# Two layers of linear attention and MLP on one core: program order from loops replaced by order from a table

## The chip, the cores and the metric

The kernel runs on 1 core of one Trainium2 chip. The metric is the device time of one execution in microseconds (us), as the median of several runs. Times inside an execution come from one execution that the hardware profiler recorded. The engines are named as the profile names them: PE (TensorE, its matmuls) and PEld (its weight loads), DVE (VectorE), ACT (ScalarE), POOL (GpSimd), SP (SyncE, which here issues DMAs). Every engine works off its own instructions in the order of the program, and waits for the others where it needs their data or their buffers.

## The reference, cut to what matters

Two layers follow each other. Each is an attention part and an MLP part, with S = 2048 rows, D = 448 columns, 16 heads of 28 and F = 1792 hidden columns, all in f32.

```python
def attention(x, wqkv, wo):                # x: 2048 x 448
    q, k, v = heads(x @ wqkv)              # 16 heads of 28
    phi = lambda t: where(t > 0, t + 1, exp(t)) + 1e-6
    pq, pk = phi(q), phi(k)
    kv = einsum("bhsd,bhse->bhde", pk, v)  # one 28 x 28 matrix a head
    z = einsum("bhsd->bhd", pk)
    num = einsum("bhqd,bhde->bhqe", pq, kv)
    den = einsum("bhqd,bhd->bhq", pq, z)[..., None] + 1e-6
    return merge(num / den) @ wo

def mlp(x, w1, b1, w2, b2):
    return gelu(x @ w1 + b1) @ w2 + b2

for layer in range(2):
    x = x + attention(layernorm(x), wqkv, wo)
    x = x + mlp(layernorm(x), w1, b1, w2, b2)
```

## The kernel before, in words

**Precision.** PE multiplies float32r operands. To keep f32 precision every operand is split into a high part (a rounded copy, on ACT: xh, kh, qh, yh, gh) and a low part (the difference, on DVE or POOL: xl, kl, ql, yl, gl), and each product is three matmuls: high by high, high by low, low by high. So every step of PE has a chain of a copy and a subtraction ahead of it.

**Tiles.** Rows are worked on in 16 tiles of 128. The first stage of a layer does for each tile t: statistics of the layer norm on DVE (`ln_stats`, L188 to L192), their inverse root on POOL (L194), the normalization on DVE (L367), and the transposition of the tile. The first 6 tiles of layer 0 are transposed on PE (`transpose_x`, L239: T0 to T5; the last 64 columns come doubled from a "tail" copy on ACT, L371); the others go through 32 x 32 transposes on DVE, a store of two tiles to DRAM as a square (`store_sq`, sq_a) and four DMAs that read it back spread out (`spread`, sp). The transposed tile is split (XH, XL). Then PE makes the key projection K(t) (`proj`, L290 to L294, 11 matmuls of 448 columns, into one of two banks "m") and the query projection Q(t) (the same lines, banks "h"). phi is relu and exp on ACT and a combination on DVE (L300 to L303). Queries are stored to DRAM (pq_d). Keys are split (kh L419, kl L420) and added up for z (za, L424). G(t) (`stage_g`, L446 to L450, 11 matmuls) adds x^T k of the tile to four banks "acc"; from the sum G the matrices kv are made later, so the values v are never formed row by row.

**Order of the first stage.** A string of tokens per tile sets the order (STEP, and STEP_0 for tile 0): `STEP = "a qp K T X s n G kp tu kh bg Q sp"`, with G one tile late, so that on PE it reads K(t), T(t+1), G(t-1), Q(t). In layer 0 this begins K0 T1 Q0 K1 T2 G0 Q1. Beside it the weights of the MLP are loaded and split in 30 background pieces (`bg_pieces`, 24 of them in this stage of layer 0, with their low halves on POOL).

**Crossing to the MLP.** When G is complete, the string ORDER sets one sequence: the last Q and G(15), z, the copies of G (gt, L558 and L560), kv (`trans_kv`), its masking, the product with wo (m), its split (Mh, Ml), and for the four tiles of block 0 the division by the denominator, the transposition (tq), the product with M (o), the residual, the layer norm and its transposition. The queries 10 to 15 (Q) are spread between these as filling for PE: Q10 stands ahead of the last G, the others behind it.

**MLP.** Four tiles make a block of 512 rows; there are four blocks of 14 steps. Step i of a block is f(i) (`mlp1`: 11 matmuls of 512 columns, L716 to L720, then gelu on ACT L722, the copy gh L725 and the subtraction gl L726) and y(i) (`mlp2`: 12 matmuls of 448 columns, L734 to L736). The loop emits f(i+1) ahead of y(i), from f(0). At the start of block 0 `trans_chunks` copies M by 14 small DMAs on SP into the place of the query weights (the step called mc in the changed kernel). The strings PLAN_0, PLAN_1 and PLAN put the attention of the next block behind these steps, among them one product oc (11 matmuls, L668 to L671) for each tile. In the last block of layer 0, the weights and the first tiles of layer 1 are prepared (steps 2 to 12).

**Buffers.** Every kind of tile has a ring of buffers (9 for x, 5 halves "S" for squares and loads, 3 for "e", 2 for most others), and the banks of PSUM are 4 "acc", 2 "h" and 2 "m"; who waits for a buffer follows from the order of the program.

Of the kernel before, what the change touches and what calls it, by code (L numbers as in the profile page):

```python
# [12 lines left out]
OP = mybir.AluOpType  # L13

# [8 lines left out]
def linear_attn_mlp_kernel(  # L23
# [19 lines left out]
    NB = NT // 4  # L43
# [11 lines left out]

    def dram(shape, dt, name):
        return tc.dram_tile(shape, dt, name=name)

# [3 lines left out]
    def bank(tag, bufs, name):  # L62
        return psum.tile([128, 512], F32, name=name, tag=tag, bufs=bufs)

    NH = 9

    def t448(tag, bufs, name, dt=F32):
        bufs = NH if tag == "H" else bufs
        return work.tile([128, D], dt, name=name, tag=tag, bufs=bufs)

    def t512(tag, bufs, name, dt=F32):
        return work.tile([128, 512], dt, name=name, tag=tag, bufs=bufs)

    def f(ap):
        return ap.bitcast(F32)


    xt = {}

    def load_x(l, t):  # L80
        xt[l, t] = t448("H", 8, f"x{l}_{t}")
        sp.dma_start(xt[l, t], x_d[l][t * 128:(t + 1) * 128, :])

    load_x(0, 0)

    wkq = {}

    def stage_piece(src, c, eng, s):

        if c < 3:  # L90
            eng.dma_start(s, src[c * 128:(c + 1) * 128, :])
        else:
            eng.dma_start(s[0:64], src[TL:D, :])
            eng.dma_start(s[64:128], src[TL:D, :])
        return s

    def load_kq(name, col):
        src = wqkv[:, col:col + D]
        st = [work.tile([128, 1024], F32, name="stg", tag="S", bufs=5) for h in range(2)]
        return [stage_piece(src, c, (sp, act)[c % 2], st[c // 2][:, c % 2 * 512:c % 2 * 512 + D]) for c in range(4)]  # L100

    def stage_square(src):

        st = []
        for h in range(2):
            s = work.tile([128, 1024], F32, name="stg", tag="S", bufs=5)[:, :2 * D]
            s = s.rearrange("p (c n) -> p c n", c=2)
            if h == 0:
                sp.dma_start(s, src[:256, :].rearrange("(c p) n -> p c n", p=128))
            else:  # L110
                sp.dma_start(s[:, 0], src[256:TL, :])
                sp.dma_start(s[:64, 1], src[TL:, :])
                sp.dma_start(s[64:, 1], src[TL:, :])
            st += [s[:, 0], s[:, 1]]
        return st

    def piece(name, i):
        return t448(f"{'W' if name == 'k' else 'V'}{i}", 1, f"w{name}{i}", F32R)

    def split_hi(name, c, st):  # L120

        if c < 3:
            wkq[name, c] = piece(name, c), piece(name, 3 + c)
            act.copy(wkq[name, c][0], st[c])
        else:
            wkq[name, 3] = piece(name, 6)
            tmps[name] = t512("e", 3, "sx", F32R)[:, :D]
            act.copy(tmps[name][64:128], st[3][64:128])
            act.copy(wkq[name, 3][0:64], st[3][0:64])

    tmps = {}

    def split_lo(name, c, st):

        eng = pool if c == 1 else dve
        if c < 3:
            hi, lo = wkq[name, c]
            eng.tensor_tensor(lo, st[c], f(hi), op=OP.subtract)
        else:
            eng.tensor_tensor(wkq[name, 3][64:128], st[3][64:128], f(tmps.pop(name)[64:128]), op=OP.subtract)  # L140

    def split_piece(name, c, st):
        split_hi(name, c, st)
        split_lo(name, c, st)

    def split_kq(name, st):
        for c in range(4):
            split_piece(name, c, st)

    st_k = load_kq("k", D)  # L150
    load_x(0, 1)
    st_q = load_kq("q", 0)
    load_x(0, 2)


    ident = consts.tile([128, 128], F32, name="ident")
    make_identity(nc, ident)
    warm = bank("m", 2, "warm")
    for i in range(20):
        pe.transpose(warm[:, :128], ident, ident)  # L160
    mhalf = consts.tile([128, 1], F32, name="mhalf")
    pool.memset(mhalf, -0.5)
    tiny = consts.tile([128, 1], F32, name="tiny")
# [20 lines left out]


    def ln_stats(xs):
        st = work.tile([128, 6], F32, name="bst", tag="bst", bufs=2)
        dve.bn_stats(st, xs)  # L188
        mv = work.tile([128, 2], F32, name="bmv", tag="bmv", bufs=2)
        dve.bn_aggr(mv, st)  # L190
        ve = work.tile([128, 1], F32, name="bve", tag="bve", bufs=2)
        dve.tensor_scalar(ve, mv[:, 1:2], 1e-5, None, op0=OP.add)  # L192
        rs = work.tile([128, 1], F32, name="brs", tag="brs", bufs=2)
        pool.tensor_tensor(rs, ve, mhalf, op=OP.pow)  # L194
        return xs, mv, rs

    def ln_norm(stats, name, twice=True):

        xs, mv, rs = stats
        xn = t512("xn", 2, name)  # L200
        dve.tensor_scalar(xn[:, :D], xs, mv[:, 0:1], rs, op0=OP.subtract, op1=OP.mult)  # L201
        if twice:
            dve.tensor_scalar(xn[:, D:], xs[:, TL:], mv[:, 0:1], rs, op0=OP.subtract, op1=OP.mult)
        return xn

    class Block:
        def __init__(self):
            self.hi = work.tile([128, 2048], F32R, name="XH", tag="XH", bufs=2)  # L210
            self.lo = work.tile([128, 2048], F32R, name="XL", tag="XL", bufs=2)

        def pieces(self, t):

            s = slice(t * 512, (t + 1) * 512)
            return self.hi[:, s], self.lo[:, s]

        def moving(self, x, c):

            return x.rearrange("p (t c n) -> p t c n", t=4, c=4)[:, :, c]  # L220

        def still(self, x, t, c):

            return x[:, (t * 4 + c) * 128:(t * 4 + c + 1) * 128]

    blocks = {}

    def block(key):
        if key not in blocks:
            blocks[key] = Block()  # L230
        return blocks[key]

    tps = {}

    def transpose_x(xn, key, j, tail=None, tag="m"):
        block(key)
        tp = tps[key, j] = bank(tag, 2, "tp")
        for c in range(4):
            pe.transpose(tp[:, c * 128:(c + 1) * 128],  # L239
                         tail if tail is not None and c == 3 else xn[:, c * 128:(c + 1) * 128], ident)  # L240

    def split_x(key, j):
        tp = tps.pop((key, j))
        hi, lo = blocks[key].pieces(j)
        act.copy(hi, tp)
        dve.tensor_sub(lo, tp, f(hi))

    squares, stored, spreads = {}, {}, {}

    def half(name):
        return work.tile([128, 1024], F32, name=name, tag="S", bufs=5)

    def turn(x, key, t):
        x = x[:, :D]
        if (key, t // 2) not in squares:
            squares[key, t // 2] = half("sq")  # L260
        sq = squares[key, t // 2].rearrange("p (m c u n) -> p c m u n", m=4, c=4, n=32)[:, :, :, t % 2]
# [4 lines left out]
    def store_sq(key, h):  # L266
        d = stored[key, h] = dram([128, 1024], F32, f"sq_{'_'.join(map(str, key))}_{h}")
        sp.dma_start(d, squares.pop((key, h)))

    def spread(key, h):  # L270
        r = spreads[key, h] = half("sp")
        d = stored.pop((key, h)).rearrange("(i r) (m f) -> m r i f", i=4, m=4)
# [3 lines left out]
    def split_t(key, t, hi, lo):  # L276

        x = spreads[key, t // 2].rearrange("p (i c u n) -> p u c i n", i=4, c=4, n=32)[:, t % 2]
        h = hi.rearrange("p (c i n) -> p c i n", c=4, n=32)
        act.copy(h, x)  # L280
        dve.tensor_sub(lo.rearrange("p (c i n) -> p c i n", c=4, n=32), x, f(h))  # L281


    def proj(name, key, j):
        ps = bank("m" if name == "k" else "h", 2, "ps" + name)
        o = ps[:, :D]
        b = blocks[key]
        for c in range(3):
            hi, lo = wkq[name, c]
            pe.matmul(o, b.still(b.hi, j, c), hi, start=(c == 0), stop=False)  # L290
            pe.matmul(o, b.still(b.hi, j, c), lo, start=False, stop=False)  # L291
            pe.matmul(o, b.still(b.lo, j, c), hi, start=False, stop=False)  # L292
        pe.matmul(o, b.still(b.hi, j, 3), wkq[name, 3], start=False, stop=False)
        pe.matmul(o, b.still(b.lo, j, 3), wkq[name, 3], start=False, stop=True)  # L294
        return o

    def phi(o, name, into=None):

        e = t512("e", 3, name)[:, :D]
# [151 lines left out]

# [284 lines left out]

    PLAN_0 = (
# [176 lines left out]
```

## Time and profile before

| | |
|---|---|
| median of 3 runs | 900.35 us (897.8 to 900.79) |
| span of the profiled execution | 899.3 us |
| PE busy | 880.1 us, 98% |
| DVE busy | 501.6 us, 56% |
| ACT busy | 342.1 us, 38% |
| POOL busy | 203.3 us, 23% |
| first matmul of K0 | 10.16 us |
| last G of layer 0 begins | 115.93 us |
| first MLP matmul of layer 0 | 151.23 us |
| K0 of layer 1 begins | 457.80 us |
| first MLP matmul of layer 1 | 590.12 us |
| last matmul begins | 895.32 us |

The profiled execution took 899.3 us from its first to its last instruction; its time as a run is not recorded by itself, and the median of the runs lies 1.05 us above that span. Busy times count work and not waiting; the ends of matmuls are modelled, so a block of PE is better measured from its first start to the next block's first start. In a row of the timeline stand the start, the duration, the engine, the line, the operation with the program's names, the shape, and in square brackets how long the engine had been idle and who ended that. In a row of a group stand the count, the busy time, the mean in ns, and the idle time before with what ended it.

### The profile page before, as it was taken

To read this page: it belongs to the slowest core of one execution; us is meant where nothing else is said; L and a number is where in the kernel's file an instruction comes from. 1 tells how busy PE (TensorE), PEld (TensorE's weight loads), DVE (VectorE), ACT (ScalarE), POOL (GpSimd) and SP (SyncE) were. 2 spreads that over 40 slices of the span, in tenths; PEclk is the share of its full clock that TensorE was granted. 3 is DMA by queue.
4 is the path that set the end of the run, shared out by engine and by line. 5 is a ranking of instruction groups with operands and counts; after the bars stand their busy time and mean duration, and the time that the engine had idled before them with its cause. 6 is when DMAs were issued, how large, how long until landed. Compare 5 with 4: busy or idle time off the path is not lost.

```text
span 899.3 us, 11664 instructions
## 1 busy us (share of the span) xinstructions
PE 880.1 (98%) x4184; PEld 771.9 (86%) x4184; DVE 501.6 (56%) x970; ACT 342.1 (38%) x590; POOL 203.3 (23%) x239
## 2 busy tenths in 40 slices
PE   7999999999999999999999999999999999999998
PEld 5888988888788888888889999788888888888887
DVE  5888686764754634226469956864665563532112
ACT  4666744322322331324345564343132233222222
POOL 2466733432112102001013223320220310210000
PEclk9999999999999999999999999999999999999999
DMA  5376631634323322051135542154134233020001
GB/s 163 103 224 228 192 117 49 206 99 125 131 70 112 101 74 70 25 174 48 48 111 189 173 142 67 47 157 132 58 99 145 79 103 129 26 69 20 22 1 42
DMA packets 62762, 93.71 MB, mean 104 GB/s; under 512 B 8816, under 2 KB 57968, under 8 KB 62704
## 3 DMA queue, kind: packets, MB, share of 16 engines
q1 hardware_dynamic: 62096, 92.05, 32.3%
q10 hardware_dynamic: 608, 0.92, 0.3%
q8 instruction: 33, 0.54, 0.3%
q14 instruction: 25, 0.20, 0.1%
HBM read 55.65 MB, written 34.08 MB: 100 GB/s over the span
## 4 chain that ended last, share of the span: by engine, by line
PE 83%; DVE 7%; DMA 3%; ACT 2%; issue 2%; SPq 1%; POOL 1%; ACTq 0%; DVEq 0%; POOLq 0%
PE y L736 10%; PE y L734 10%; PE y L735 10%; PE hp L718 8%; PE hp L717 8%; PE hp L716 8%; PE hp L720 3%; PE hp L719 3%; PE G L447 2%; PE G L448 2%; PE G L446 2%; PE psk L292 2%; PE psk L290 2%; PE op L669 2%; PE psk L291 2%
## 5 line engine op out<-in xcount | busy, mean ns | idle before, releaser
L726 DVE TENSOR_TENSOR gl<-g,gh 128x512 fp32r<-128x512 f32 x112 | 79.5, 710 | 305.1 <-ACT gh L725 305.1
L722 ACT ACTIVATE g<-hp,b1s 128x512 f32<-128x512 f32 x112 | 77.1, 688 | 398.7 <-PE hp L720 394.9
L734 PE MATMUL y<-w2h,gh 128*128 128x448 f32 x448 | 163.8, 366 | 1.7 <-ACT g L722 1.7
L736 PE MATMUL y<-w2h,gl 128*128 128x448 f32 x448 | 163.8, 366 | 0.8 <-DVE gl L726 0.8
L735 PE MATMUL y<-w2l,gh 128*128 128x448 f32 x448 | 163.6, 365 | 0.0
L718 PE MATMUL hp<-XL,w1h 128*128 128x512 f32 x336 | 131.3, 391 | 0.3 <-DVE XL L281 0.3
L716 PE MATMUL hp<-XH,w1h 128*128 128x512 f32 x336 | 131.5, 391 | 0.1
L717 PE MATMUL hp<-XH,w1l 128*128 128x512 f32 x336 | 131.6, 392 | 0.0
L194 POOL TENSOR_TENSOR brs<-bve,mhalf 128x1 f32<-128x1 f32 x64 | 39.3, 614 | 324.3 <-DVE bve L192 318.3
L734 PEld LDWEIGHTS y<-w2h,gh 128*128 128x128 f32 x448 | 84.1, 188 | 11.4 <-ACT g L722 2.5
L735 PEld LDWEIGHTS y<-w2l,gh 128*128 128x128 f32 x448 | 84.1, 188 | 8.4
L736 PEld LDWEIGHTS y<-w2h,gl 128*128 128x128 f32 x448 | 84.2, 188 | 7.8 <-DVE gl L726 1.2
L718 PEld LDWEIGHTS hp<-XL,w1h 128*128 128x128 f32 x336 | 63.1, 188 | 14.8 <-DVE XL L281 1.2
L716 PEld LDWEIGHTS hp<-XH,w1h 128*128 128x128 f32 x336 | 63.1, 188 | 11.8 <-ACT XH L280 0.8
L717 PEld LDWEIGHTS hp<-XH,w1l 128*128 128x128 f32 x336 | 63.1, 188 | 11.2
L725 ACT CAST gh<-g 128x512 fp32r<-128x512 f32 x112 | 69.7, 622 | 3.6
L619 POOL TENSOR_TENSOR pz<-pq,zb 128x448 f32<-128x448 f32 x32 | 36.7, 1148 | 105.3 <-DVE dn L625 74.4
L188 DVE BATCH_NORM_STATS2 bst<-x 128x6 f32<-128x448 f32 x64 | 39.8, 622 | 10.0 <-DMA x<-in_A_x_dram 8.9
L683 POOL TENSOR_TENSOR x<-x,b2b 128x448 f32<-128x448 f32 x32 | 36.9, 1152 | 31.5 <-DVE xm L201 23.3
L719 PE MATMUL hp<-XH,w1x 128*128 128x512 f32 x112 | 43.6, 389 | 0.0
L720 PE MATMUL hp<-XL,w1x 128*128 128x512 f32 x112 | 43.6, 389 | 0.0
L400 POOL TENSOR_TENSOR xnl<-x,xnh 128x384 fp32r<-128x384 f32 x32 | 35.9, 1122 | 28.9 <-ACT xnh L399 22.4
(144 smaller groups left out, 1575.7 us busy)
## 6 DMA issues: line engine op xcount, KB each, us to landing
x<-in_A_x_dram SPq DMA_DIRECT2D x32, 224.0 KB, 3.8
pq_d<-eq SPq DMA_DIRECT2D x32, 224.0 KB, 2.9
pq<-pq_d SPq DMA_DIRECT2D x32, 224.0 KB, 3.2
x<-x_d SPq DMA_DIRECT2D x32, 224.0 KB, 3.4
sq_a<-sq SPq DMA_DIRECT2D x13, 512.0 KB, 2.6
sp<-sq_a SPq DMA_DIRECT2D x52, 128.0 KB, 3.0
sq_q<-sq SPq DMA_DIRECT2D x12, 512.0 KB, 2.6
sp<-sq_q SPq DMA_DIRECT2D x48, 128.0 KB, 3.0
```

The costliest lines, as they stand in the source:

```text
L188: dve.bn_stats(st, xs)
L716: pe.matmul(o, w1h[:, c, s], x.moving(x.hi, c), start=(c == 0), stop=False)
L717: pe.matmul(o, w1l[:, c, s], x.moving(x.hi, c), start=False, stop=False)
L718: pe.matmul(o, w1h[:, c, s], x.moving(x.lo, c), start=False, stop=False)
L719: pe.matmul(o, w1x[:, s], x.moving(x.hi, 3), start=False, stop=False)
L720: pe.matmul(o, w1x[:, s], x.moving(x.lo, 3), start=False, stop=True)
L722: act.activation(g, hp, AF.Gelu_apprx_tanh, bias=b1s[:, i:i + 1])
L725: act.copy(gh, g)
L726: dve.tensor_sub(gl, g, f(gh))
L734: pe.matmul(acc[j], gh[:, s], w2h[:, i], start=first, stop=False)
L735: pe.matmul(acc[j], gh[:, s], w2l[:, i], start=False, stop=False)
L736: pe.matmul(acc[j], gl[:, s], w2h[:, i], start=False, stop=last)
```

## The change

The loops, STEP, ORDER, PLAN and their helper functions go. Every step becomes a small named operation, registered by a decorator, and takes the layer, a number and, if wished, an engine. One text for each layer lists all of them in the order of the program:

```diff
+    T = {}
+    ops = {}
+
+    def op(fn):
+        ops[fn.__name__.rstrip("_")] = fn
+        return fn
+
+    ENG = {"a": act, "d": dve, "p": pool, "s": sp}
...
+    def run(l, text):
+        for tok in text.split():
+            up = (tok[0] == ">") - (tok[0] == "<")
+            tok, _, e = tok.lstrip("<>").partition(":")
+            name = tok.rstrip("0123456789")
+            ops[name.replace("_", "")](l + up, int(tok[len(name):] or 0), e)
+
     for l in range(LAYERS):
...
+        run(l, ORDER[l])
```

A token such as `wql1:p` is step wql (the low part of the query weights), number 1, on POOL; `>` ahead of it means the next layer. Names: ld, a, ar, n, d (load, statistics, root, normalization and tail of a tile), wkld, wkh, wkl and wqld, wqh, wql (load, high and low part of a piece of the key and query weights), T, tu, st, sp (transposition on PE; on DVE, its store and its spread), xh and xl, sh and sl (split of the transposed and of the plain tile), K, ke, kp, kh, kl, za, Q, qe, qp, qs, G (as above; ke is relu and exp, kp the combination), bld, bhi, blo (load, high and low part of a background piece), z, zb, dc, gt, kv, mask, m, mh, ml, mc (crossing), pl, pz, pd, pm, pT, pu, ps, pp, qh, ql, o, oc, oa (queries and attention output), la, ln, lx, lb, mT, mu, ms, mp, yh, yl (norm and transposition ahead of the MLP), f, g, gh, gl, y, u (the MLP; u is one tile's part, three matmuls, of a y), ya, ys (residual and store). The text of layer 0 begins:

```diff
+        "ld0 a0 ld1 a1 wkld0 wkld1:a wkld2 wkld3:a wqld0 wqld1:a wkh1 wkl1:p wkh3 ar0 n0 d0 wkh0 ar1 n1 d1 wkl3 "
+        "warm20 wqld2 ld2 wkl0 T0 xh0 xl0 wkh2 wqld3:a tab0 T1 xh1 wqh0 wqh2 sh0 wkl2 K0 xl1 K1 ke0 a2 ar2 wql0 "
+        "wqh1 wql1:p n2 wql2 d2 T2 kp0 wqh3 wql3 Q0 kh0 kl0 ld4 ld3 a4 a3 ke1 sl0 G0 qe0 qp0 qs0 kp1 kh1 xh2 ar4 "
+        "ar3 n3 bld2:xn d3 za0 n4 xl2 za1 kl1 sh1 Q1 qe1 K2 ke2 qp1 ld6 a6 T3 sl1 G1 bld0:xn bhi0 blo0 ld5 a5 ar5 "
```

around the crossing to the MLP of layer 0 (a line here leaves out the tokens between)

```diff
+        "xl15 K15 pl2 pl3 qs9 wv1 ke14 kp14 kh14 kl14 za14 G13 ke15 kp15 za15 sh15 sl15 kh15 bhi21 kl15 G14 G15 "
+        "gt1 gt0 blo21 wv0 pl1 bld22:xn ld0 pl0 gt3 z gt2 zb bhi20 dc pz1 pd1 pm1 Q10 kv bhi22 qe10 qp10 qs10 Q11 "
...
+        "bld24:W6 qs15 f0 g0 bhi24 f1 g1 gh0 pd4 pm4 gl0 blo24 pz5 lb3 f4 f2 bld25:W5 gh1 tab1 bhi25 g2 lb0 u3 u1 "
+        "f3 u2 u0 gl1 y1 pd5 pm5 pu4 pu5 g4 gh2 gh4 mc ld7 pl6 blo25 pz6 pd6 gl2 y2 f6 pl7 pz7 ps2 g3 gh3 gl4 gl3 "
```

and from the end of layer 0 to layer 1

```diff
+        "ya13 ys12 >sh0 >tab0 >wkl1:p >K0 >ke0 >sl0 lb14 >kp0 ya14 lb15 >sh1 >ld10 ys13 >ld5 >a5 >kh0 >kl0 >sl1 "
+        ">ar5 ya15 >za0 >n5 >ld6 ys14 >a6 >Q0 >ar6 >n6 >tu5 >ld8 >st2 >ld7 >Q1 >K1 >ke1 >kp1 >tu6 >G0 >K2 >qe0 "
```

On PE the new order of layer 0 begins T0 T1 K0 K1 T2 Q0 G0 Q1 K2 T3 G1. Q10 stands behind G15 in layer 0 and ahead of it in layer 1. In layer 0's MLP f0 f1 f4 f2 come ahead of the first y. The preparation of layer 1 (weights, and tiles 0 to 8) stands in the last block of layer 0, and its first stage begins K0 Q0 Q1 K1 G0 K2.

What each step computes, its lines of arithmetic, the rings of buffers and the banks stay as they were. One step is new, a one-column activation by relu (tab0) or gelu (tab1), each once in a layer:

```diff
+    @op
+    def tab(l, n, e):
+        act.activation(spare, mhalf, AF.Gelu_apprx_tanh if n else AF.Relu)
```

Two more of the new functions, which show the manner in which a step of the loops was cut up:

```diff
-    def stage_kh(l, t, za):
...
+    @op
+    def kh(l, t, e):
+        T["kh", l, t] = ring("E", 512, "kh", F32R)[:, :D]
+        T["kl", l, t] = ring("F", 512, "kl", F32R)[:, :D]
+        act.activation(T["kh", l, t], T["K", l, t], AF.Identity, bias=tiny)
+
+    @op
+    def kl(l, t, e):
+        dve.scalar_tensor_tensor(T["kl", l, t], T["K", l, t], 1e-6, f(T["kh", l, t]), op0=OP.add, op1=OP.subtract)
```

More of the change, by code (lines that the diff above doesn't have):

```diff
@@ L714, in mlp1, with f_ @@
+    def f_(l, n, e):
+        b, i = divmod(n, NF)
+        hp = T[l, "hp", n] = bank(e or "h", "hp")
+        s = rows(i)
+        x = block("m", l, b)
         o = hp.rearrange("p (t n) -> p t n", t=4)
```

1074 lines of the change are left out of this document (470 added, 604 removed), and 85 rows, old and new, of the table ORDER.

## The prediction

> **What bounds the kernel now.** I read the page first, then the list of who waited for whom on PE, then the timeline of PE.
>
> ```profile
> span 899.3 us, 11664 instructions
> ...
> PE 880.1 (98%) x4184; PEld 771.9 (86%) x4184; DVE 501.6 (56%) x970; ACT 342.1 (38%) x590; POOL 203.3 (23%) x239
> ```
>
> PE bounds it: it is busy 98% of the span. The multiset of instructions is the same before and after but for four one-column activations, so PE's work cannot shrink; only waits can go or come. A busy PE here is modelled, so I measure a block from its start to the next one's start:
>
> ```profile
> 701.60 0.37 PE L734 MATMUL y<-w2h,gh 128*128 128x448 f32 x1
> 704.04 0.39 PE L716 MATMUL hp<-XH,w1h 128*128 128x512 f32 x1
> 706.56 0.36 PE L668 MATMUL op<-wq,qh 128*128 128x448 f32 x1
> 708.78 0.37 PE L734 MATMUL y<-w2h,gh 128*128 128x448 f32 x1
> ```
>
> Without waits a y block (12 matmuls) takes 2.44 us, an f block 2.52, an eleven-matmul block of 448 columns (op; K, Q and G are of the same size) 2.22. So a quarter of a microsecond lost is visible. The waits of PE (total, times, longest):
>
> ```profile
> PE tp L239 <- ACT tail L371: 1.8, 1, 1.8
> PE y L734 <- ACT g L722: 1.7, 2, 0.9
> PE tp L239 <- DVE x L367: 1.4, 2, 1.0
> ...
> PE G L447 <- DVE kl L420: 1.3, 2, 0.7
> PE psq L290 <- ACT wq L124: 1.1, 1, 1.1
> ...
> PE y L736 <- DVE gl L726: 0.8, 1, 0.8
> PE G L446 <- ACT kh L419: 0.7, 1, 0.7
> ...
> PE G L448 <- POOL xnl L400: 0.7, 1, 0.7
> ```
>
> These eight sum to 9.5 us, in small pieces at three kinds of place: the start (tail, x, wq), the first stage of each layer (G), and the beginning of an MLP (y). That is the stock on which the change can draw: about 1% of the time.
>
> **The start, step by step.**
>
> ```profile
> 4.39 1.21 SPq L91 DMA_DIRECT2D stg<-in_A_wqkv_dram  x2
> ...
> 5.29 0.55 POOL L194 TENSOR_TENSOR brs<-bve,mhalf 128x1 f32<-128x1 f32 x1 [2.79 <-DVE bve L192]
> ...
> 5.88 0.51 DVE L367 TENSOR_SCALAR x<-x,bmv,brs 128x448 f32<-128x448 f32 x1 [0.67 <-POOL brs L194]
> ...
> 6.07 0.47 ACTq L94 DMA_DIRECT2D stg<-in_A_wqkv_dram  x1
> ...
> 6.58 1.28 ACT L124 ACT_TABLE_LOAD   x1 [6.58 <-DMA stg<-in_A_wqkv_dram]
> ...
> 8.81 0.29 ACT L371 COPY tail<-x 128x128 f32<-128x128 f32 x1
> ...
> 8.98 1.13 POOL L138 TENSOR_TENSOR wk<-stg,wk 128x448 fp32r<-128x448 f32 x1 [3.13 <-ACT wk L124]
> ...
> 10.16 0.47 PE L290 MATMUL psk<-wk,XH 128*128 128x448 f32 x1 [0.68 <-ACT XH L245]
> ...
> 11.43 0.57 PE L290 MATMUL psk<-wk,XH 128*128 128x448 f32 x1
> ...
> 11.80 0.57 PE L291 MATMUL psk<-wk,XH 128*128 128x448 f32 x1
> ...
> 25.57 0.36 PE L290 MATMUL psq<-wq,XH 128*128 128x448 f32 x1
> ```
>
> Added wait: on POOL the low half of chunk 1 of the K weights now stands ahead of tile 0's inverse root (brs), so that root, the normalization, the tail copy and the transposes T0 queue behind it. I take chunk 1 to be there by 4.4, when SP issues later pieces. From there one DMA issue on ACT (0.47), the table load (1.28) and the copy (0.5) end at 6.7, POOL's 1.13 at 7.9, the root's 0.55 at 8.5. Then, as before, the normalization (0.57 with the hop), from the tail copy to the first matmul 1.35 (8.81 to 10.16), and between them one weight copy (0.5): K0 at 10.9 instead of 10.16, **+0.75**. K0's matmuls were 0.37 apart (11.43, 11.80), half the steady pace; I keep that. Then the order K0 K1 T2 Q0 G0 pays: before, PE stood 1.1 for wq and 1.0 for tile 2's normalization; now K1 lies over the splitting of wq and over tile 2's statistics. K0 ends at 14.6, K1 at 16.9, T2 at 17.3, Q0 at 19.55, G0 at 21.8; before, the same work ended at 25.57 (where Q1 starts). **-3.7.**
>
> The Trainium skill, page "TensorE: Matmul & The Clock Gate", Part 1, says that an idle window of about 3.4 us drops the clock to half until the next window. The 0.37 spacing agrees. The new order leaves PE idle from the warm-up's end to T0 for some 3 us, as the old one did; by that rule nothing is added unless a second window falls, and then 2.7 us would be.
>
> **The first stage of layer 0.** DVE is the second engine here (stretch; busy time of PE, PEld, DVE, ACT, POOL):
>
> ```profile
> 25.00:100.00 75.00, 72.51 (x358) 65.42 (x357) 59.78 (x122) 51.31 (x102) 46.29 (x54) 1.00 0.65 201
> ```
>
> ```profile
> L419 ACT ACTIVATE kh<-psk,tiny 128x448 fp32r<-128x448 f32 x32 | 20.4, 636 | 35.8 <-DVE psk L303 35.8
> ...
> L303 DVE SCALAR_TENSOR_TENSOR psk<-psk,ek 128x448 f32<-128x448 f32 x32 | 20.1, 628 | 18.2 <-ACT ek L301 18.2
> ...
> L420 DVE SCALAR_TENSOR_TENSOR kl<-psk,kh 128x448 fp32r<-128x448 f32 x32 | 19.8, 618 | 10.3 <-ACT kh L419 9.8
> ...
> L301 ACT ACTIVATE ek<-ek 128x448 f32<-128x448 f32 x32 | 18.5, 579 | 1.0
> ```
>
> ```profile
> 56.71 0.36 PE L290 MATMUL psk<-wk,XH 128*128 128x448 f32 x1
> ```
>
> From K(t) to G(t) the chain is two activations of at most 0.58, then 0.63, 0.64 and 0.62: 3.0 us, some 3.4 with the hops. Before, three blocks (6.7 us) covered it, now two (4.4) for most tiles: still covered, with 1 us to spare, if DVE is free. Walking DVE's new order with these rows I find two late places: K2 waits for tile 2's low half, which stands behind the statistics of tiles 4 and 3 and two normalizations (about 1 us), and K7 needs the bank of K5, which the sum of keys releases, and that waits on DVE behind a split (1.3 us). Against that go the old waits of G for kl (1.3) and kh (0.7). At K6 (56.71 before) the walk stands at 53.5, and at the last G it is about 4 us ahead.
>
> ```profile
> sp<-sq_a SPq DMA_DIRECT2D x52, 128.0 KB, 3.0
> ```
>
> On SP the load of weight piece 8, which waits for POOL to release a buffer (about 56.8 in my walk), now stands ahead of the four spreads for tiles 8 and 9. Four issues of 0.6 (the two at 4.39 took 1.21) and 3.0 to land give 62, and K8 needs them at 67. Hidden, with 5 us to spare.
>
> **Between the stages.** One block, Q10, moves from before the last G to behind it:
>
> ```profile
> 115.93 0.72 PE L446 MATMUL G<-kh,xnh 128*128 128x448 f32 x1
> ...
> 118.82 1.16 DVE L560 COPY gt<-G 128x448 f32<-128x448 f32 x2 [0.21 <-PE G L450]
> ...
> 151.23 0.40 PE L716 MATMUL hp<-XH,w1h 128*128 128x512 f32 x1
> ```
>
> ```profile
> 118.82:151.23 32.41, 31.24 (x175) 26.71 (x174) 28.73 (x60) 11.68 (x23) 10.03 (x11) 1.00 0.13 47
> ```
>
> From the copy of G to the first f block 32.4 us pass, and DVE is busy 28.7 of them with the same work in both kernels: this stage belongs to DVE, and PE's order in it changes little. What counts is when it begins. The last G starts at 109.7 (115.93 less 4 and less the 2.2 of Q10). I add the 2.9 from there to the copy and the 32.4 as before, and 0.7 for two instructions on dc that used to run ahead of the copies (about 1.4 in all, estimated from the 448-column rows above, half of it into DVE's old gaps): first f at about 145.7, **-5.5 in all so far**.
>
> **The MLP of layer 0.**
>
> ```profile
> L726 DVE TENSOR_TENSOR gl<-g,gh 128x512 fp32r<-128x512 f32 x112 | 79.5, 710 | 305.1 <-ACT gh L725 305.1
> ...
> L722 ACT ACTIVATE g<-hp,b1s 128x512 f32<-128x512 f32 x112 | 77.1, 688 | 398.7 <-PE hp L720 394.9
> ...
> L725 ACT CAST gh<-g 128x512 fp32r<-128x512 f32 x112 | 69.7, 622 | 3.6
> ```
>
> Four f blocks (10 us) now stand ahead of the first y, so the chain gelu, copy, subtraction (0.69, 0.62, 0.71) is covered several times over. The waits for g (0.9 of the 1.7) and for gl (0.8) go, and 0.3 of smaller ones. The 14 small copies that rebuild the projection (mc) move behind w2's next pieces on SP. Two copies on ACT (qh and yh) that stand ahead of g13 and g17 wait for spreads; in the walk both have 2 us to spare. **-2.0.**
>
> **Layer boundary and layer 1.** G0 of layer 1 waited 0.7 for its low half on POOL; Q1 and K1 now lie between, and a hop beside it goes. **-1.0.** Stage and crossing of layer 1 keep their order in the main (Q10 stays ahead of the last G): **0**, bounded by -1.5 (the rest of the waits listed) and +3 (two more places like K7). MLP of layer 1: the second wait for g, 0.9, and a hop of 0.3: **-1.2**. Tail: the same four adds and stores: 0.
>
> **Function tables.** The changed program holds four table loads at the same places (first copy; first exp of layer 1; twice the first gelu). The new one-column activations ask for relu, or for gelu after a gelu; they cost ACT four instructions of at most 0.3 us (the tail copy, 128 columns, takes 0.29), hidden by ACT's 62% of idle time, and bring nothing. The Trainium skill, page "ScalarE: Activation LUTs", section "Table sets: the hidden batching unit", says that relu is in every set: by it too, asking for relu loads no exp table. By its "What ACT_TABLE_LOAD costs" a switch takes 2.66 us with a drain, against the 1.28 of the row; that alters no term, as these loads lie under cover.
>
> **Sum.** -5.5 - 2.0 - 1.0 + 0 - 1.2 = -9.7 us on the span of 899.3: 889.6. The median of the runs, 900.35, lies 1.05 above that span, so **890.7 us**.
>
> **Rivals.**
> 1. *Part of it is given back on DVE.* K2 and K7 are two of some 30 such places. If in-order waits of 0.5 us come at ten of them, it is 895.7. For: DVE is busy 59.8 of 75 us. Against: the old order had the same load. 0.18.
> 2. *The start goes wrong*: chunk 1 lands late, or PE idles once more and runs 16 more matmuls at half pace (0.17 each): 2.7 back, 893.4. In the forecast's range, and counted with it.
> 3. *Nothing moves*: the two stages are limited by DVE and the small waits reappear at the next instruction. 900.35. For: the crossing of layer 1 is such a stage. 0.10.
> 4. *Slower.* One mechanism: DVE's queue in the first stages. A tile takes PE three blocks, 6.7 us; with 59.8 of 75 DVE idles 1.4 us of them. With two blocks of cover instead of three, each wait of DVE on ACT (for ek 18.2 us, for kh 9.8 in all) can end last. It uses up the gain at 9.7/32 = 0.3 us per tile over the 32 tiles; at 0.5 per tile the time is 890.7 + 16 = 906.7. Against: my walk of layer 0 found 2.3 us over 16 tiles, already in the sum. 0.10.
> 5. *All waits go*, also those at K2 and K7 and the 1.5 of layer 1: about 4 us better, 886.7, at best 884. 0.06.
>
> **How the numbers follow.** Forecast (with 2) 0.56, rivals 0.18, 0.10, 0.10, 0.06. About 0.3% (2.7 us) is what a measurement of this kernel tells from no change: faster is below 897.6. Faster: 0.56 + 0.16 of rival 1 + 0.06 = 0.78; same: 0.02 + 0.10 = 0.12; slower 0.10. The range takes in the +3 and -1.5 of layer 1, rivals 1, 2 and 5, and ends short of no change: 884 to 899, which leaves out rivals 3 and 4, 2 in 10.
>
> **What would show it.** K0 at about 10.9 and Q1 at about 22; a wait of about 1 us at K2; the first f at 145.7; no wait of y for g; four table loads. A first f later than 149 means that the first stage failed; waits of G or K for DVE above 5 us in all mean rival 1 or 4. A new wait of PE for ACT behind a DMA inside an MLP would be something that I did not see.

## The result and the profile after

| | before | changed |
|---|---|---|
| median | 900.03 us (897.8 to 900.79, 4 runs) | 885.99 us (885.57 to 887.83, 4 runs) |
| span of the profiled execution | 899.3 us | 884.4 us |

The ratio is 0.9852 (95% interval 0.9837 to 0.9867): by the medians it is 14.0 us less, where 9.7 had been forecast. By the spans of the two profiled executions it is 14.9. Where a run's time and the span of the same execution are both on record, the time is 1.7 us above the span (886.11 and 884.4), so the profiled execution of before was one of the longer ones, about 901.0 by this estimate. The page and the list of PE's waits of the changed kernel, to be held against those of before:

```profile
span 884.4 us, 11576 instructions
...
PE 873.2 (99%) x4184; PEld 773.2 (87%) x4184; DVE 473.7 (54%) x970; ACT 337.0 (38%) x594; POOL 203.8 (23%) x239
```

```profile
PE tp L382 <- DVE x L353: 2.8, 1, 2.8
PE y L828 <- DVE gl L818: 1.5, 1, 1.5
PE warm L221 <- POOL tiny L175: 1.4, 1, 1.4
PE psk L492 <- DVE za L538: 0.8, 1, 0.8
PE psq L492 <- DVE eq L507: 0.6, 1, 0.6
PE tq L686 <- DVE kvm L617: 0.3, 1, 0.3
```

Of the eight waits quoted in the prediction none of the G's, no wait for wq and none for g is left. At the start the waits for the tail copy (1.8) and for x (1.4) have become one wait for x, of 2.8. Three are new: for gl2 in the first block of the MLP, for the sum of keys (za) and for eq in layer 1. And DVE, with the same 970 instructions, is busy 27.9 us less. That was not foreseen, and some of the experiments are about it.

Stage by stage for each kernel: the stretch, its length, and the busy time of PE, PEld, DVE, ACT and POOL. The borders are the first Q1, the last G of layer 0, the first f block, K0 of layer 1, its last G, its first f block. Before:

```profile
0.00:25.57 25.57, 18.60 (x76) 14.56 (x77) 14.71 (x31) 12.47 (x24) 8.50 (x23) 0.93 0.47 144
25.57:115.93 90.36, 87.87 (x434) 79.50 (x432) 68.32 (x134) 61.80 (x121) 56.23 (x65) 1.00 0.64 196
115.93:151.23 35.30, 34.13 (x188) 29.19 (x187) 30.16 (x62) 13.31 (x25) 12.03 (x13) 1.00 0.17 59
151.23:457.80 306.57, 304.69 (x1421) 266.37 (x1420) 153.02 (x293) 98.72 (x159) 49.02 (x49) 1.00 0.30 96
457.80:554.74 96.94, 96.28 (x466) 86.86 (x464) 72.81 (x138) 53.91 (x97) 30.31 (x43) 1.00 0.49 156
554.74:590.12 35.38, 34.05 (x189) 29.20 (x187) 30.04 (x62) 13.31 (x25) 11.42 (x12) 1.00 0.13 45
590.12:899.30 309.18, 304.51 (x1421) 266.26 (x1419) 132.50 (x254) 88.56 (x139) 35.78 (x36) 1.00 0.24 77
```

Changed:

```profile
0.00:21.29 21.29, 16.92 (x77) 14.77 (x78) 13.14 (x30) 12.51 (x25) 8.61 (x22) 0.92 0.44 140
21.29:106.03 84.74, 84.74 (x421) 77.54 (x420) 64.57 (x135) 60.80 (x118) 50.66 (x62) 1.00 0.68 207
106.03:141.88 35.85, 35.85 (x200) 31.64 (x199) 29.47 (x62) 14.60 (x28) 13.04 (x13) 1.00 0.28 92
141.88:446.86 304.98, 303.47 (x1421) 266.62 (x1420) 146.03 (x291) 96.78 (x162) 54.22 (x53) 1.00 0.30 96
446.86:544.09 97.23, 95.78 (x466) 86.97 (x464) 66.50 (x140) 54.17 (x99) 29.32 (x44) 1.00 0.52 163
544.09:577.35 33.26, 32.98 (x187) 29.19 (x186) 27.43 (x62) 11.55 (x22) 9.75 (x12) 1.00 0.13 43
577.35:884.40 307.05, 303.44 (x1421) 266.47 (x1419) 126.51 (x253) 86.61 (x140) 38.22 (x37) 1.00 0.23 76
```

In the second stretch PE is busy for its whole length, 84.74 of 84.74. Q10 (2.22) and the small product for z (0.40) moved from this stretch into the next, so the lengths are compared with 2.62 taken from the one and given to the other:

| stage | forecast | measured | lost on PE, before and changed |
|---|---|---|---|
| start, to Q1 | -3.7 | -4.3 | 9.5 and 5.3 |
| first stage of layer 0, without Q10 and z | -0.3 | -3.0 | 2.9 and 0 |
| crossing of layer 0, with them | -1.5 | -2.1 | 2.0 and 0.3 |
| MLP of layer 0 | -2.0 | -1.6 | 3.7 and 1.9 |
| boundary, first stage and crossing of layer 1 | -1.0 | -1.8 (+0.3 and -2.1) | 3.8 and 2.2 |
| MLP of layer 1 and tail | -1.2 | -2.1 | 2.5 and 0.2 |
| sum | -9.7 | -14.9 | 24 and 10 |

The last column adds up, over all matmuls of a stage, the time from one start to the next, less the median of that time for its kind (good to some 0.3 us a stage). In every stage PE lost less than before by about what the stage became shorter: the gain is time that PE no longer loses, everywhere. About half of it stands in the list of waits; the rest is in shorter pauses and in matmuls at half the clock.

### The profile page after: what moved, and what is told of

Its sections match the earlier page's. It is cut to its first block, busy times and chain, and to the rows that moved or that the text cites. A ratio compares the mean times of both kernels' runs of the same rounds, so it can differ in the third digit from the quotient of the medians.

```text
span 884.4 us, 11576 instructions
## 1 busy us (share of the span) xinstructions
PE 873.2 (99%) x4184; PEld 773.2 (87%) x4184; DVE 473.7 (54%) x970; ACT 337.0 (38%) x594; POOL 203.8 (23%) x239
## 4 chain that ended last, share of the span: by engine, by line
PE 93%; DVE 3%; DMA 2%; ACT 1%; issue 0%; POOL 0%; SPq 0%; ACTq 0%; POOLq 0%; DVEq 0%
PE y L828 10%; PE y L827 10%; PE y L826 10%; PE hp L800 9%; PE hp L799 9%; PE hp L801 9%; PE hp L802 3%; PE hp L803 3%; PE psk L492 2%; PE G L567 2%; PE G L568 2%; PE G L566 2%; PE psk L494 2%; PE psk L493 2%; PE psq L493 2%; PE psq L494 2%
## 5 line engine op out<-in xcount | busy, mean ns | idle before, releaser
L665 POOL TENSOR_TENSOR pz<-pq,zb 128x448 f32<-128x448 f32 x32 | 38.7, 1212 | 100.2 <-DVE dn L670 57.2
L484 POOL TENSOR_TENSOR xnl<-x,xnh 128x384 fp32r<-128x384 f32 x32 | 33.6, 1051 | 68.3 <-ACT xnh L210 48.0
L744 DVE TENSOR_TENSOR x<-op,x 128x448 f32<-128x448 f32 x32 | 19.8, 620 | 51.6 <-PE op L738 50.8
L420 DVE TENSOR_TENSOR XL<-sp,XH 128x512 fp32r<-128x512 f32 x50 | 35.8, 728 | 18.8 <-ACT XH L210 18.8
```

## The experiments

The theory: PE bounds everywhere, and what is won at one place is kept to the end; the extra gain of the first stage comes from DVE, which is held up less by POOL. The rivals: DVE bounds the first stages and takes early gains back; PE's order alone did it; a wait that goes comes back at the next late instruction; the function tables did it. In each set of four runs the kernels shared the runs of the kernel before, so ratios to before are compared: 0.1% is 0.9 us, and each ratio is good to some 0.15%. Between sets more caution is needed: the changed kernel itself came out at 0.9852 here and at 0.9826 in the last set, with the same median (885.99 and 886.02 us), since the kernel before took 900.0 in the one and 902.4 in the other. So a difference of less than 2 us to the changed kernel is read from the stages of the profile as well. For one and the same order the stages differ in steadiness: the crossing of layer 0 took 35.8 to 35.9 us in all profiles, but the stretch from K6 to the last G 54.2 to 55.5.

**The old start.** The first 85 steps of layer 0 in the order of before:

```diff
+OLD_START = "ld0 wkld0 wkld1:a wkld2 wkld3:a ld1 ... T0 xh0 xl0 n1 d1 wkh2 wkl2 wkh3 wkl3 ... K0 T1 ... Q0 ... K1 T2 ... G0 ... Q1"
+ORDER = (OLD_START + the remaining steps of ORDER[0], ORDER[1])
```

> The changed kernel with the start of layer 0 (up to G0 and Q1) in the order of the kernel before on all engines; the rest is as changed. Theory A: PE is the bound from there on, so what the start gains is kept to the end: G0 of tile 0 ended 4.3 us earlier in the changed kernel (21.3 against 25.6), and without the new start the time rises by 4.0 to 4.5 us, to about 890.3. Theory B: the first stage and the crossing belong to DVE, which catches up when it starts late: the rise is 0 to 2 us. If the first f block comes 4 us later than 141.9, A holds.

Measured: 891.93 us, ratio 0.9908 (0.9893 to 0.9923) against 0.9852, about 5 us more by the ratio and 6 by the medians. The first f block began at 146.41 instead of 141.88, 4.5 later, just what the start had given: theory A holds. The profiled execution (span 890.8) lost 2.7 us more in the MLP of layer 0 (307.72 from the first f block to K0 of layer 1, against 304.98), in its first block:

```profile
PE y L852 <- DVE gl L842: 2.6, 1, 2.6
```

That is the new wait for gl2, 1.1 us longer than in the changed kernel, of which more below. The rest is the clock: behind this wait it was granted at 0.50 (third number from the right) for about 3.4 us, and half of these are lost.

```profile
168.00:170.00 2.00, 2.00 (x7) 1.74 (x6) 0.00 (x0) 0.00 (x0) 0.00 (x0) 0.50 0.96 246
```

**Q10 ahead of the last G.**

```diff
-kl15 G14 G15 ... pd1 pm1 Q10 kv
+kl15 G14 Q10 G15 ... pd1 pm1 kv
```

> The changed kernel with one token moved: Q10 of layer 0 stands ahead of the last G again. The prediction counted Q10 as filling under a crossing that DVE bounds: then the time rises by about 1.5 us (2.2 less 0.7), to 887.5. Rival, from the two profiles: the crossing of layer 1, where Q10 stayed ahead, became 2.1 us shorter as well, and PE has no long gaps in either, so PE bounds it and the place of Q10 is worth nothing: 886.0 within 0.4, with the first f block at 141.9 as before.

Measured: 888.0 us, ratio 0.9862 (0.9845 to 0.9878), some 0.9 us more by the ratio and 2.0 by the medians. From the first G (19.56) to the first f block (143.89) it took 124.33 instead of 122.83 (19.05 to 141.88): 1.5 more, the prediction's number. Of these 1.3 lie in the crossing, the steady part: it took 34.91 (108.98 to 143.89), where 35.85 less the 2.22 of Q10 would be 33.6. The list of waits shows 0.8 of it:

```profile
PE mp L639 <- DVE kvm L632: 0.8, 1, 0.8
```

Behind the last G, Q10 and Q11 fill the time in which G is copied and kv is masked; ahead of it, Q10 leaves part of that time empty. The rival (nothing) is out for layer 0.

**A longer warm-up.**

```diff
-warm20
+warm32
```

> The changed kernel with 32 instead of 20 transposes in the warm-up, which then end at about 8.7 instead of 5.9, just ahead of the first transposes of x at 8.8. Theory A: the 0.37 spacing of K0's first matmuls comes from the clock, granted at 0.50 from 10 to 13 after PE stood idle for 2.8; without the idle time the clock stays full, K0 takes about 1 us less, and the time falls by 0.5 to 1.2 us, to about 885.2. Theory B: K0 waits for its operands (the low half of chunk 2 at 11.8, XL at 11.2) or the next waits take up what is won: no change, 886.0 within 0.3.

Measured: 885.56 us, ratio 0.9838 (0.9823 to 0.9853): by the medians 0.4 us less, which is not clear of the spread. The clock granted (third number from the right) in the changed kernel, and then with the longer warm-up:

```profile
10.00:12.00 2.00, 1.90 (x5) 1.24 (x5) 1.99 (x4) 2.00 (x6) 0.00 (x0) 0.50 0.44 123
12.00:14.00 2.00, 2.00 (x9) 1.78 (x8) 1.79 (x5) 0.74 (x2) 0.55 (x1) 0.66 0.03 10
```

```profile
10.00:12.00 2.00, 1.72 (x6) 1.16 (x7) 2.00 (x4) 2.00 (x6) 0.00 (x0) 1.00 0.41 117
12.00:14.00 2.00, 2.00 (x12) 1.85 (x11) 1.67 (x5) 1.28 (x4) 0.67 (x1) 1.00 0.00 1
```

So the slow pace was the clock: K1 began at 13.11 instead of 14.15. The first G began 1.0 us earlier and K6 too (50.82 against 51.86), but the last G did not (106.36 against 106.03). In this one profile the microsecond was lost again between K6 and the last G (55.54 instead of 54.17). The three later runs with the longer warm-up took 54.4 to 55.2 there, the others with this order 54.2 to 54.8: some of the microsecond is lost again, and how much varies from run to run.

**gl2 ahead of the scaling of tile 6.**

```diff
-blo25 pz6 pd6 gl2 y2
+gl2 blo25 pz6 pd6 y2
```

> The changed kernel with one token moved: in block 0 of layer 0's MLP the low half gl2 stands ahead of the scaling of tile 6 (pd6) instead of behind it. In the changed kernel PE waits 1.5 us for gl2 at 159.5, and DVE had stood 4.3 us for pd6, whose data (pl6) are loaded behind the 14 small copies of mc on SP. Theory A: that is the only reason for the wait; the time falls by 1.5 us, to 884.5. Theory B: the wait moves to the next low half or to y3, since ACT and the two buffers of gh are late too: 0 to 0.5 us, 885.7.

Measured: 884.79 us, ratio 0.9833 (0.9819 to 0.9848). From the first f block to K0 of layer 1 303.19 us instead of 304.98: 1.8 less, and no wait of y for gl is left. Theory A holds. The timeline of the changed kernel shows the chain that the edit breaks (SP, POOL, DVE, PE):

```profile
144.82 1.24 SPq L646 DMA_DIRECT2D wq<-Mh  x2
...
154.83 0.91 SPq L660 DMA_DIRECT2D pq<-pq_d  x2
...
157.70 1.16 POOL L665 TENSOR_TENSOR pz<-pq,zb 128x448 f32<-128x448 f32 x1 [5.39 <-DMA pq<-pq_d]
...
158.90 0.62 DVE L670 TENSOR_REDUCE dn<-pz 128x16 f32<-128x448 f32 x1 [4.27 <-POOL pz L665]
...
159.93 1.96 DVE L818 TENSOR_TENSOR gl<-g,gh 128x512 fp32r<-128x512 f32 x2
...
161.34 0.47 PE L828 MATMUL y<-w2h,gl 128*128 128x448 f32 x1 [1.51 <-DVE gl L818]
```

The 14 copies of mc take SP from 144.8 to 154.2 to issue; the load of tile 6's queries (pl6) stands behind them, POOL's product behind the load, DVE's reduction behind that, and gl2 behind the reduction and two small instructions of pd6. DVE idled 4.27 us; in the run with the edit gl2 ran at 157.79, 2.1 us earlier and before POOL's product was there. A part of the wait is of another kind: the row of gl stands for two, and the first, gl2, ended just ahead of PE's start at 161.34, so it took 1.35 us, beside POOL's next product, against 0.69 in the run with the edit (the last section tells of that).

**Dummies on POOL**, behind 18 inverse roots, wide and narrow:

```diff
+    def dum(l, n, e):
+        for i in range(2):
+            pool.tensor_tensor(wide, ones, ones, op=OP.subtract)                        # wide: 128x128
+            pool.tensor_tensor(wide[:, :1], ones[:, :1], mhalf, op=OP.pow)              # narrow, in its place
```

> The changed kernel with work added on POOL that nobody needs: behind the inverse root of tiles 5 to 15 in layer 0's first stage and of tiles 9 to 15 in layer 1's stand two subtractions of 128 x 128 (about 1.0 us together), just when DVE normalizes the tile from SBUF to SBUF. Theory A: such a DVE instruction runs about twice as long while POOL works on a wide tile (0.51 to 1.2 us), so 18 normalizations become 0.4 to 0.7 us longer, DVE's busy time rises by about 8 us, and PE waits for it again in the first stage of layer 0: the time rises by 1 to 4 us more than with the narrow dummies. Theory B: DVE and POOL do not disturb each other, and the shorter DVE times of the changed kernel have another reason: no more than POOL's own delay, the same as with the narrow ones.

> The control: the same 18 places, but two powers of one column (0.6 us each by the roots of the profile, 1.2 us together). POOL is taken for as long, and its next work comes as late, but there is hardly any data. Theory A: DVE's instructions keep their length (19 of 19 that ran beside a root did in the changed kernel), and the time rises by 0 to 1 us only. Theory B: the same as with the wide ones.

Measured: wide 889.08 us, ratio 0.9868 (0.9854 to 0.9882), narrow 888.64, 0.9864 (0.9851 to 0.9877): equal, and more than the changed kernel by 1 us (ratios) to 3 us (medians). The wide dummies did not do what they were made for: the normalizations kept a median of 512 ns, and DVE's busy time rose by 1.6 us, not 8. Nine normalizations ran beside a wide dummy and none of them was more than 0.1 us longer: in the kernel before a stretched normalization ended some 0.25 us after the POOL instruction beside it, and a dummy of 0.4 us is over too soon to stretch one of 0.51. So these two runs say what a delay of POOL costs in the first stage of layer 0 (the last G at 107.4 and 107.7 instead of 106.0), and do not decide between the theories on DVE.

**The split of x later, in the kernel before.**

```diff
-    STEP = "a qp K T X s n G kp tu kh bg Q sp"
+    STEP = "a qp K T X n G kp s tu kh bg Q sp"
```

> The kernel before with one token moved in the order of a tile: the split of x (copy on ACT, subtraction on POOL) stands behind the combination of phi instead of ahead of the normalization, so that POOL subtracts while DVE works on PSUM or transposes. DVE's own order and PE's order stay. Theory A: the stretched DVE instructions of the first stages (6.7 and 9.1 us too long in all) fall to less than half, and with them the waits of G for kh and kl in layer 0: the time falls by 1 to 3 us, to about 898. Theory B: the gain of the first stage came from PE's new order alone: 900.0 within 0.5.

Measured: 899.19 us, ratio 0.998 (0.997 to 0.9991): 1.8 us less, between 0.8 and 2.7. The page, and the normalization in the kernel before, in this one and in the changed one (count: shortest, median, longest in ns):

```profile
PE 881.1 (98%) x4184; PEld 775.9 (86%) x4184; DVE 488.9 (54%) x970; ACT 342.8 (38%) x590; POOL 197.5 (22%) x239
```

```profile
L367 DVE TENSOR_SCALAR x<-x,bmv,brs x32: 503/930/1215, 5.9 to 513.7; 128x448 f32<-128x448 f32 x32
```

```profile
L367 DVE TENSOR_SCALAR x<-x,bmv,brs x32: 503/509/1208, 5.9 to 513.5; 128x448 f32<-128x448 f32 x32
```

```profile
L353 DVE TENSOR_SCALAR x<-x,bmv,brs x32: 503/512/1348, 8.2 to 501.8; 128x448 f32<-128x448 f32 x32
```

One token took 12.7 us off DVE's busy time (501.6 to 488.9), and the time fell by 1.8. The first stage of layer 1 became 1.7 us shorter (458.49 to 553.70 against 96.94), and in layer 0 from the first G to the last 0.7 (91.97 against 92.68), which one execution of each hardly tells from nothing. This profiled execution lost 1.7 us at its start (Q1 at 27.29 against 25.57), because the granted clock was 0.50 there from 9.7 to 23.4 and not for 3.4 us only; the two stretches lie behind that. Theory A has its sign and a size within its range: in the two first stages the stretched DVE instructions fell to less than half. But with DVE's stalls gone, less than 1 of the 3 us of the first stage of layer 0 is explained.

**No one-column activations.**

```diff
-tab0 (twice), tab1 (twice)
```

> The changed kernel without its four one-column activations. Theory: they load no table that the next activation would not have loaded at the same place, and lie under idle time of ACT: 886.0 within 0.3, four table loads. Rival: they bring the gelu's table load forward, and without them each layer loses up to 1.3 us at the first gelu or exp: 887 to 889.

Measured: 888.35 us (886.24 to 889.48), ratio 0.9857 (0.9841 to 0.9874). The four table loads of 1.28 us stand where they stood. By the medians that is 2.4 us more than the changed kernel, as the rival said. But the profiled run was 3.4 us longer than that of the changed kernel, 2.9 of them in the MLP of layer 0, with this wait:

```profile
PE y L845 <- DVE gl L835: 2.9, 1, 2.9
```

In this execution one pair of mc's copies took 2.98 us to issue instead of 1.23, and everything behind it on SP came that much later. The wait is 1.4 us longer than in the changed kernel, and the other 1.5 are again the clock, at 0.50 for 3.4 us behind it. In the run with the old start one pair took 2.88, with the wait of 2.6. So the wait for gl2 varies from run to run with SP's queue, and a comparison of single edits on this kernel is blurred by it. The last set removes it.

**The changed kernel again, and four edits at its remaining waits** (warm32 and gl2 as above, and in layer 1):

```diff
-kp5 xl7 xl6 a12 ... kl5 n11 za5 G4
+kp5 xl7 xl6 za5 a12 ... kl5 n11 G4
->ke1 >kp1 >tu6 >G0 >K2 >qe0 >za1 >kh1 >sh2 >qp0
+>qe0 >ke1 >qp0 >kp1 >tu6 >G0 >K2 >za1 >kh1 >sh2
```

> The changed kernel itself once more, beside the three that follow, so that they are compared with it on one chip: 886.0 within 1.5; its own runs spread by 2 us, by the theory because the wait for gl2 at the start of layer 0's MLP depends on when a load lands behind 14 small copies.

> The changed kernel with four edits, one at each of PE's remaining waits: 32 transposes in the warm-up; gl2 ahead of pd6 in layer 0's MLP; in layer 1 the sum of keys za5 ahead of the normalization of tile 11 (PE waits 0.8 for it at K7) and phi of Q0 ahead of that of K1 (PE waits 0.6 for it at Q2). Theory A (PE bounds everywhere, each wait is paid in full): 1.5 + 0.8 + 0.6 and about 0.5 of the warm-up, 3.4 less than the changed kernel, 882.5. Theory B (a wait that goes comes back at the next late instruction): 1.5 less at most, 884.5.

Measured: the changed kernel 886.02 us, ratio 0.9826 (0.9812 to 0.9839); four moves 884.03, 0.9804 (0.979 to 0.9817). Two microseconds, not 3.4. Those of gl2 are kept: 303.19 us from the first f block to K0 of layer 1, as in the run with gl2 alone, against 305.38. In layer 1 both waits are gone and two others have come:

```profile
PE psk L510 <- DVE kl L547: 0.6, 1, 0.6
PE G L584 <- ACT kh L543: 0.6, 1, 0.6
```

From K0 to the first f block of layer 1 it is 130.9 us as against 130.6. Theory A holds for the MLP, theory B for the first stage of layer 1.

**Q10 of layer 1 moved too; and four moves without the activations.**

```diff
-wv1 pl3 Q10 qe10 za15 ... gt1 Q11 pd1 pm1 pm0 gt0 kv mask pT0
+wv1 pl3 za15 ... gt1 Q10 pd1 pm1 pm0 gt0 kv qe10 mask Q11 pT0
```

> The same, and Q10 of layer 1 moved behind the last G as in layer 0 (and Q11 behind kv). Theory A: what it brought in layer 0, 1.5 us at the first f block in the run with Q10 moved back, it brings here too: 1 to 1.5 less than with four moves. Theory B: in layer 1 PE waits only 0.3 for kvm in this crossing, so there is no more than 0.5 to be had.

> The four moves without the four one-column activations. The run without them on the changed kernel was 1 to 2 us slower, but its profile showed that in the wait for gl2 (2.9 us instead of 1.5), which hangs on a DMA. Theory A: that wait was the whole difference; with gl2 moved the activations are worth nothing, and this kernel is equal to the one with four moves within 0.4. Theory B: the activations do help, by bringing a table load forward: 1 to 2 us slower than with four moves.

Measured: five moves 885.06 us, 0.9812 (0.9799 to 0.9825), 1 us more and not less; PE now waits 0.9 for kh at a G and 0.5 for the last za ahead of z. In the profile 0.8 of the 1.3 us more lie in the first stage of layer 0, where the two orders are the same, and 0.5 from K0 to the first f block of layer 1. So the move gained nothing; that Q10 ahead of the last G fills the time until the last keys are ready is likely by the wait for za, and not shown further. Four moves without the activations 884.09 us, 0.9799 (0.9786 to 0.9813), equal to 884.03: with the wait for gl2 out of the way the activations are worth nothing that these runs can tell. The version with four moves beats both kernels (883.79 to 885.92 against 885.69 to 888.22 for the changed one).

## Why the prediction was right, and where it was off

The time fell the way that was forecast and lies in the range, but not where the forecast put most of its chance: 885.99 is the place of rival 5, which had 0.06, and its mechanism came true in the main: no wait at K2 and K7, and less time in layer 1's crossing.

*The bound and the stock.* Right: PE's work is the same, and only its waits moved. Of the eight waits that the prediction listed (9.5 us) those at G, wq and g are gone. But these eight were not the stock. The page of before shows 19.2 us in which PE was idle (899.3 less 880.1), and from start to start PE lost 24 us; so a gain of 14.9 was possible where "about 1% of the time" was taken as all.

*The start, -3.7.* Right in mechanism, measured -4.3, and the run with the old start shows that it is kept to the end. K0 came at 10.27 and not at 10.9: the table load on ACT began at 4.61, where the forecast had 4.87 (before 6.58, when more DMA issues stood ahead of it on ACT), and from the tail copy (8.77) to K0 it took 1.50 and not 1.85, as the weight copy between them added 0.15 and not 0.5.

*The first stage of layer 0, -0.3.* This is the step that failed in size: -3.0. The walk of DVE's queue found K2 1.0 late and K7 1.3 late, and neither wait came; without these 2.3 us the step would have been -2.6. The walk took the normalization at its mean, 0.88 us (the recorded text does not give the length it used). The row by source above shows that this mean is of two kinds, 0.50 and up to 1.2, with the median at 0.93; ahead of K2 there stand two of them, and in the changed kernel each took 0.50, which is 0.8 of the 1.0. Tile 2's low half was ready at 23.6 (22.89 and 0.68), 0.1 us after K2 began and before its third matmul needs it:

```profile
22.47 0.50 DVE L353 TENSOR_SCALAR x<-x,bmv,brs 128x448 f32<-128x448 f32 x1
22.89 0.68 DVE L418 TENSOR_TENSOR XL<-tp,XH 128x512 fp32r<-128x512 f32 x1
...
23.52 0.36 PE L492 MATMUL psk<-wk,XH 128*128 128x448 f32 x1
...
23.92 0.36 PE L494 MATMUL psk<-wk,XL 128*128 128x448 f32 x1
```

For K7 the sum of keys ended at 53.4, and K7 began at 54.1 without a wait. Which instructions are long is set by what POOL does beside them, and so by the order, the thing that was changed. PE lost nothing from Q1 to the last G, where it had lost 2.9. How much of that is DVE's shorter instructions and how much the order on PE and ACT is not separated: with DVE's stalls alone removed, the kernel before gained 0.7 in this stage, so most of it is likely the order, but no run takes the new order with the old stalls.

*Q10 and the crossing, -1.5.* Right in number: -2.1 measured, and 1.5 in the run that moved Q10 back. But the reason, "this stage belongs to DVE", was wrong, and the number came in part by luck: in the changed kernel PE is busy 35.85 of 35.85 there, and the prediction's own row of before has PE at 31.24 of 32.41, above DVE's 28.73. In layer 1 the crossing gained 2.1 without any move of Q10, against 0 forecast (bounded by -1.5): the new order inside it shortened the wait for kvm and removed those for ql and xm (together about 1 us of a layer), and PE's loss there fell from 2.1 to 0.4, the rest in shorter pauses.

*The MLP of layer 0, -2.0.* The old waits went as forecast, but a new one of 1.5 came, and it is the kind that the prediction named as not seen: a wait behind a DMA, only through POOL and DVE instead of ACT. The prediction noted that mc's 14 copies move behind w2's loads and did not count their own issues, 9.4 us of SP, nor what is queued behind them. Without that wait the step is -3.4 (303.19 against 306.57), so the -2.0 was near the measured -1.6 only because one term too small and one left out offset each other.

*Layer 1, -1.0, and its MLP, -1.2.* Signs right. The 0.7 at the boundary went and 0.6 and 0.8 came at Q2 and K7, the "places like K7" of the bound. The MLP of layer 1 lost its two waits (0.9, and three gaps of 0.2 to 0.3 at the same place); some 0.6 us of its -2.1 is not in the list of waits, but PE's loss from start to start fell from 2.5 to 0.2 there.

*Function tables.* Right: four loads at the same places, and nothing lost without the activations.

*The rivals.* DVE as a new bound (rivals 1 and 4) was priced by DVE's busy time of before, 59.8 of 75 us; that time itself fell, to 57.6 in the same 75 us of the changed kernel, in which PE did 373 matmuls and not 358. Rival 5, all waits gone, 886.7 to 884, is nearest to what came, though three small new waits stand. The step from span to run time, 1.05, was too small: it is 1.7 where both are on record.

## What to carry to other kernels

Take the stock of what an engine can win from start to start of its instructions and not from a list of waits: the list had 9.5 us, and 24 were lost. Look at the spread of a group (shortest, median, longest) before its mean goes into a walk: a mean between two kinds of durations fits neither, and a new order changes how many there are of each. When a step with many small DMAs moves, add up its issues on the queue and follow what is behind them through every engine that stands in order. On an engine that is 99% busy, edit for edit is kept only where the next instructions have slack: one token in the MLP gave all it promised, two in a tight stage gave nothing.

## What the runs showed of the hardware that was not expected

DVE is held up by POOL on data in SBUF, and who starts first decides. I counted each of DVE's 298 normalizations, scalings and splits with all tiles in SBUF, against the median of its kind with no POOL instruction beside it. In the kernel before, 92 overlapped a wide POOL instruction (64 columns or more). In 72 of these POOL had started first: 65 took over 0.1 us longer, by 0.63 us in the mean. In the 20 where DVE had started first, none did, and none of the other 206 did either, among them 24 that ran beside a one-column root only. In the changed kernel it was 38 of 47, 1 of 16 and none of 235. In sum these instructions were 41.3 us too long before and 22.9 after; in the two first stages 7.0 and 9.3 before, 2.3 and 2.0 after, and 2.8 and 1.1 in the run with the split of x later. That is 18 of the 27.9 us by which DVE's busy time fell. The split of the transposed x shows the same from its two sources (from SBUF after a spread, and from PSUM), in the kernel before:

```profile
L281 DVE TENSOR_TENSOR XL<-sp,XH 128x512 fp32r<-128x512 f32 x50 | 38.8, 780 | 1.1 <-ACT XH L280 1.1
...
L246 DVE TENSOR_TENSOR XL<-tp,XH 128x512 fp32r<-128x512 f32 x14 | 9.4, 682 | 2.2 <-ACT XH L245 2.1
```

The Trainium skill, page "SBUF — State Buffer", section "Who interferes with whom", says that DVE and GpSimd share one pair of ports as an exclusive lock: whoever comes second waits for the whole instruction, and a DVE instruction with both inputs in SBUF is subject to it against a GpSimd instruction that reads SBUF. The rows of the split agree, and so does the count by who started first; the normalization reads one tile only, and that sentence does not speak of it. The one-column root differs from it: it takes some 0.6 us and held up none. What a lock costs a kernel bound by PE is another matter: 12.7 us of DVE's time were worth 1.8 us.

The clock fell after less idle time than I had reckoned with. PE idled 2.8 us from the warm-up's end to the first transposes (the wait for x in the first list above), then worked lightly, and the granted clock was 0.50 from 10 to 12 and 0.66 from 12 to 14, in all about 3.4 us at half. With a gap of 1.1 us it stayed at 1.00. The waits for gl2 give more such gaps: behind 1.5 (the changed kernel), 1.6 (narrow dummies), 1.7 (the changed kernel again) and 1.8 us (longer warm-up) the clock stayed at 1.00; behind 1.8 (wide dummies), 2.6 and 2.9 us it fell to 0.50 for 3.4 us. So the length of a gap alone does not decide near 1.8. In the runs with Q10 moved back and with the wide dummies the profile has no record of a lower clock at the start, yet K0's matmuls were 0.37 us apart there too: the spacing is the surer sign. The prediction kept the half pace for K0, which was right; that twelve more transposes would save it lay in its own rows and was not drawn, though their worth on the whole time stays unclear (885.56 against 885.99). The Trainium skill, page "TensorE: Matmul & The Clock Gate", Part 1, speaks of an idle window of about 3.4 us that runs freely; no such window fits into 2.8 us, so here a window with some transposes at its end must have counted as idle, if that rule holds.
